# Block-sparse attention feeding a gated feed-forward layer: scores in array tiles of 64 rows from loaded queries, and another order inside a step

## The chip, the cores and the metric

The kernel runs on one core of one Trainium2 chip. The metric is device time in microseconds, from one launch of the whole program; lower is better. The kernel before was timed three times, with a median of 854.73 us (854.47 to 855.68). One further execution was recorded by the hardware profiler; all rows below are from that one.

## The reference

Attention over 4 batches, 8 heads, 768 positions and a head dimension of 64. Positions form 24 blocks of 32. A query block sees its own block and the two beside it, the first and the last block, and three sampled blocks; the first and the last query block see every key. What is not seen is masked before the softmax. The result goes through a feed-forward layer whose middle is `h * erf(softplus(h))`. All inputs are float32.

```python
scores = scale * np.matmul(q, k.transpose(0, 1, 3, 2))
mask = np.abs(blk_i - blk_j) <= 1
mask = mask | (blk_i == 0) | (blk_j == 0) | (blk_i == n_blocks - 1) | (blk_j == n_blocks - 1)
for qb in range(n_blocks):
    for kb in sampled_blocks[qb]:
        mask[qb * 32:(qb + 1) * 32, kb * 32:(kb + 1) * 32] = True
attn = softmax(np.where(mask, scores, -1e9))
x = (attn @ v), heads side by side            # 3072 tokens x 512
h = x @ w_in                                  # 512 -> 2048
sp = np.maximum(h, 0.0) + np.log1p(np.exp(-np.abs(h)))
out = (h * erf(sp)) @ w_out                   # 2048 -> 512
```

## The kernel before

**Units of attention.** The work on scores is cut into 16 units for each batch. Ten are of kind `m`: four query blocks (`t` from 0 to 4) for four heads (`quad` 0 or 1, two head pairs `r` each). Two are of kind `e`: the two query blocks before the last, again for four heads. Four are of kind `f`: the last and the first query block for one pair of heads (`pr`), against all 768 keys. The order in a batch is ten `m`, then f0, e0, f1, f2, e1, f3.

**Queries.** `load_q` brings the queries of four blocks into a tile `qt` of 128 rows: 64 rows of one head of a pair above 64 rows of the other. `order_q` copies them into `qm`, which was set to zero once: for each pair of heads and each block it holds 128 rows by 64 columns, one head's queries in the upper rows of 32 columns, the other's in the lower rows of the other 32, and zeros elsewhere. So one product over all 128 rows gives the scores of both heads.

**Scores.** In `scores`, an `m` unit makes 24 products: two head pairs, three groups of key columns (96 around the block, 96 gathered by GpSimd into `kg`, 64 of the first and last block), four blocks. Each writes 64 rows of the PSUM tile `s` (two banks, one buffer): blocks alternate between the upper and the lower 64. They are in float32, and the trace holds two weight loads and two matmuls for each product. An `e` unit makes 12 such products in one bank, an `f` unit two products of 512 and 256 columns with all 128 columns of the array.

**After the scores.** `soft_max` takes the row maxima on VectorE (`mx`, `nb`). `soft_exp` makes the exponentials on ScalarE (`pf`) and their float16 upper part, `soft_low` the lower part on VectorE (`p`). `soft_turn` has SyncE's queue turn them through DMA into `pT`. Two units later `values` multiplies them with the gathered values `vb` into `po` (one buffer): 96 products for an `m` place, 192 for the place of `f` and `e`, in four array tiles of 128 rows by 32 columns. `norm` divides on VectorE (`rinv`, `xf`). At each second place `turn` splits the result in two halves (ScalarE, then VectorE) and turns it by DMA into `xT` for the feed-forward layer.

**The feed-forward layer.** 96 groups: 12 chunks of 256 tokens by 8 groups of 256 columns. `ff_first` makes 24 matmuls of 256 columns into `h` (three buffers), `ff_logs` five passes on ScalarE, `ff_power` one on VectorE, `ff_exp` one on ScalarE, `ff_gate` three on VectorE (in the next step), `ff_second` twelve matmuls of 512 columns into `o` (two steps later).

**Order.** Every instruction stays in program order on its engine. A prologue works on the first four units while the weights are decoded. Then 98 steps follow. A table (`until`) says in which steps a unit is begun: in each of the first sixteen, after that in five or six of each eight. A step of before issues: products `h` and their passes; `values` of the unit two back; `gathers` (GpSimd copies of keys, SyncE loads of values, with block numbers that the engine reads first); `scores` and `used_keys`; `ff_gate`; `norm`; early work on the weights; `ff_second`; `soft_max`; `next_queries` (`order_q`, `load_q`); `ff_power`; `soft_exp`; `ff_exp`; stores; `turn`; `soft_low`; `soft_turn`. SyncE's queue is also in program order: within a step the loads of values, then that of queries, then the turns.

## Time and profile before

| What | Value |
|---|---|
| median of three runs | 854.73 us |
| the profiled execution's own time | 856.55 us |
| its span, from the first to the last instruction | 854.8 us |
| TensorE matmul busy | 712.1 us, 83% of the span, 11100 matmuls |
| TensorE weight loads busy | 505.2 us, 11100 loads |
| ScalarE busy | 601.0 us, 70% |
| VectorE busy | 553.7 us, 65% |
| GpSimd busy | 136.0 us, 16% |
| mean granted TensorE clock | 0.94 of full speed |

1.75 us of the execution's time lie outside its span. Busy matmul time counts the stretch from a matmul's start to a modelled end; matmuls overlap, so the time that a block takes is read from the start of one block to the start of the next. [...]

### The profile page before, as it was taken

The page shows a single profiled execution, that of the slowest core. Times are in us where ns is not written, and L with a number is a line of the kernel's source. Part 1 is how long each engine was busy: PE and PEld are TensorE (multiplying, and loading weights), DVE is VectorE, ACT ScalarE, POOL GpSimd, SP SyncE. Part 2 cuts the span into 40 slices and gives each one's busy share as a digit, 9 for nine tenths or more (in the row PEclk, how much of TensorE's full clock was granted, in tenths as well). Part 3 has the DMA queues.
Part 4 walks back from the last instruction along what each step waited for, and adds up shares of the span by engine and source line. Part 5 has one row for each costly group of instructions (what it writes and reads, how often), then busy time and mean ns, then how long its engine had stood idle before and what let it go on. Part 6 is the DMA issues. An engine that isn't in the chain of part 4 may idle for free.

```text
span 854.8 us, 26699 instructions
## 1 busy us (share of the span) xinstructions
PE 712.1 (83%) x11100; PEld 505.2 (59%) x11100; DVE 553.7 (65%) x974; ACT 601.0 (70%) x999; POOL 136.0 (16%) x350
## 2 busy tenths in 40 slices
PE   1224655877997999899999989899999899999997
PEld 1214543544675766666776666566767676666663
DVE  3947587677856466775657766766667667655453
ACT  4635556778877576796778777867777677776774
POOL 6514020111321123200113231000111100000000
PEclk9556776999999899999999999999999999999999
DMA  8986733666689988662589697831576867211000
GB/s 325 388 252 187 227 88 86 163 169 174 165 174 206 219 197 209 177 162 45 132 164 208 177 211 170 206 97 44 132 160 151 190 129 186 65 31 39 1 26 26
DMA packets 199930, 131.61 MB, mean 154 GB/s; under 512 B 144000, under 2 KB 167168, under 8 KB 199808
## 3 DMA queue, kind: packets, MB, share of 16 engines
q1 hardware_dynamic: 195520, 114.95, 55.1%
q0 software_dynamic: 4288, 14.95, 5.0%
q8 instruction: 87, 1.43, 0.7%
q14 instruction: 35, 0.29, 0.1%
HBM read 83.88 MB, written 12.95 MB: 113 GB/s over the span
## 4 chain that ended last, share of the span: by engine, by line
PE 43%; DVE 17%; ACT 13%; DMA 11%; issue 10%; SPq 2%; POOL 2%; POOLq 0%; ACTq 0%
PE h L52 17%; PE o L52 16%; PE po L52 4%; PE s_m L52 4%; ACT x L52 3%; ACT pf_m L52 3%; DMA vtab<-vn 3%; DVE mx_m L52 3%; DVE g L52 3%; DVE q L52 3%; DMA vb<-vtab 2%; ACT q L52 2%; SPq L52 2%; DVE p_m L52 2%; ACT p_m L52 2%
## 5 line engine op out<-in xcount | busy, mean ns | idle before, releaser
L52 PE MATMUL o<-wo,g 128*128 128x512 f16 x1152 | 271.0, 384 | 16.2 <-DVE wo L52 8.5
L52 PE MATMUL h<-xT,wi 128*128 128x256 f16 x2304 | 273.8, 276 | 12.4 <-DVE wi L52 8.3
L52 PEld LDWEIGHTS <-wi 128*128 128x128 f16 x2304 | 227.9, 99 | 62.6 <-DVE wi L52 9.2
L52 PEld LDWEIGHTS <-g 128*128 128x128 f16 x1152 | 110.2, 99 | 142.5 <-issue 24.6
L52 ACT ACTIVATE x<-x 128x512 f32<-128x512 f32 x288 | 181.5, 630 | 9.1
L52 POOL COPY kg<-kx 128x128 f32 x264 | 97.6, 422 | 281.7 <-PE s_m L52 176.6
L52 ACT ACTIVATE pf_m<-s_m,nb_m 128x256 f32<-128x256 f32 x160 | 62.8, 475 | 73.0 <-DVE nb_m L52 72.6
L52 DVE SCALAR_TENSOR_TENSOR q<-x,q 128x512 f32<-128x512 f32 x96 | 66.7, 694 | 61.4 <-ACT x L52 60.4
L52 ACT ACTIVATE x<-h,isg 128x512 f32<-128x512 f32 x96 | 65.3, 680 | 37.2 <-PE h L52 36.7
L52 PE MATMUL s_m<-kx,qm 128*64 128x64 f32 (+1 forms) x1280 | 74.9, 247 | 9.9 <-ACT pf_m L52 7.5
L52 ACT ACTIVATE q<-q 128x512 f32<-128x512 f32 x96 | 59.5, 619 | 29.8 <-DVE q L52 29.8
L52 DVE SCALAR_TENSOR_TENSOR q<-q,h 128x512 f32<-128x512 f32 x96 | 65.5, 682 | 22.6 <-ACT q L52 21.9
L52 DVE TENSOR_TENSOR p_m<-pf_m,p_m 128x1024 f16<-128x1024 f32 x40 | 49.3, 1233 | 38.0 <-ACT p_m L52 38.0
L52 PE MATMUL po<-vb,pT_m 128*32 128x65 f16 (+1 forms) x3840 | 43.9, 202 | 35.9 <-DMA vb<-vtab 24.2
L52 DVE SCALAR_TENSOR_TENSOR g<-q,g 128x512 f16<-128x512 f32 x96 | 66.5, 693 | 3.3
L52 PEld LDWEIGHTS s_m<-kx,qm 128*64 128x64 f32 x1280 | 59.6, 145 | 13.3 <-ACT pf_m L52 8.1
L52 PEld LDWEIGHTS <-pT_m 128*32 128x32 f16 x3840 | 38.0, 98 | 46.0 <-issue 19.0
L52 ACT ACTIVATE q<-x 128x512 f32<-128x512 f32 x96 | 60.5, 630 | 3.0
L52 DVE TENSOR_REDUCE mx_m<-s_m 128x4 f32<-128x1024 f32 x40 | 48.7, 1218 | 16.0 <-PE s_m L52 16.0
L52 PE MATMUL s_m<-kg,qm 128*64 128x96 f32 x640 | 47.7, 258 | 6.0 <-POOL kg L52 4.7
L52 DVE TENSOR_TENSOR x<-xf,x 128x512 f16<-128x512 f32 x24 | 17.1, 714 | 47.3 <-ACT x L52 47.3
L52 DVE TENSOR_SCALAR g<-q 128x512 f16<-128x512 f32 x96 | 41.4, 431 | 3.3
(111 smaller groups left out, 631.3 us busy)
## 6 DMA issues: line engine op xcount, KB each, us to landing
vb<-vtab SPq DMA_DIRECT2D x280, 65.0 KB, 2.9
vb<-vtab SPq DMA_DIRECT2D x32, 390.0 KB, 4.0
vraw<-in_v_dram SPq DMA_DIRECT2D x10, 768.0 KB, 5.2
wo<-in_w_out_dram POOLq DMA_DIRECT2D x14, 512.0 KB, 5.9
vtab<-vn SPq DMA_DIRECT2D x16, 390.0 KB, 5.6
vb<-vtab SPq DMA_DIRECT2D x12, 520.0 KB, 4.7
qt<-in_qT_dram SPq DMA_DIRECT2D x20, 256.0 KB, 3.7
out_dram<-wo SPq DMA_DIRECT2D x20, 256.0 KB, 3.9
```

Source lines behind the costliest of these rows:

```text
L52: done = call(*args, **kwargs)
```

## The change

Queries are no longer copied: `qm` with its zeros and `order_q` are gone, and `qt` has two buffers. `scores` takes each head of a pair by itself: 64 rows of `qt` (upper or lower) against 64 rows of keys, 32 queries wide (64 in an `f` unit). An `m` unit then makes 48 products in eight array tiles of 64 rows by 32 columns: the column place follows the block, the row half follows the head, and each half writes its own bank of `s`. An `e` unit makes 24 products, each pair of head and block with its own 32 rows of one bank; an `f` unit makes four, with a head's 64 rows each, both in the same banks. `values` reads its columns where the new layout puts them. `load_q` is called right after `scores`, in other units than before.

A step is also ordered otherwise. On TensorE: `h`, scores, `o`, values (before: `h`, values, scores, `o`). On VectorE: `ff_gate`, maxima, power, `soft_low`, `norm`, the split of `turn` (before: `ff_gate`, `norm`, maxima, `order_q`, power, the split of `turn`, `soft_low`). On SyncE's queue: the load of queries, the loads of values (which now follow later products), then the turns.

```diff
     qts = {}
-    qm = cp.tile([P, HP, 4, 2, BLOCK], F32, tag="qm", name="qm")
-    pool.memset(qm, 0.0)
 
     def load_q(b, t):
-        place, tag, bufs = (mo, "g", FF_LAG + 1) if b == 0 and t in (1, 2) else (ld, "qt", 1)
-        qt = place.tile([P, HP, P], F32, tag=tag, name=f"qt_{b}_{t}", bufs=bufs)
+        qt = ld.tile([P, HP, P], F32, tag="qt", name=f"qt_{b}_{t}", bufs=2)
...
-    def order_q(b, t):
-        qt = qts.pop((b, t)).rearrange("p r (j c) -> p r j c", c=BLOCK)
-        copy = act.copy if b == 0 and t in (1, 2) else dve.tensor_copy
-        for a in range(2):
-            copy(qm[a * D : (a + 1) * D, :, :, a, :], qt[a * D : (a + 1) * D])
...
-            s4 = s.rearrange("p (h r w) -> p h r w", h=2, r=2)
+            qt = qts[b, t]
+            s4 = s.rearrange("p (a r w) -> p a r w", a=2, r=2)
             for r in range(2):
                 pr = 2 * quad + r
                 for part in range(3):
                     for j in range(4):
-                        o = slice((j % 2) * 64, (j % 2) * 64 + 64)
-                        q_ = qm[:, pr, j].rearrange("p a c -> p (a c)")
-                        c, e, keys = key_columns(b, 1 + 4 * t + j, slice(0, P), pr)[part]
-                        pe.matmul(s4[o, j // 2, r, c:e], q_, keys, start=True, stop=True)
+                        o = slice(j * BLOCK, (j + 1) * BLOCK)
+                        for a in range(2):
+                            rows = slice(a * D, (a + 1) * D)
+                            c, e, keys = key_columns(b, 1 + 4 * t + j, rows, pr)[part]
+                            pe.matmul(s4[o, a, r, c:e], qt[rows, pr, o], keys, start=True, stop=True)
...
                     for j in range(2):
-                        o = slice(j * 64, j * 64 + 64)
-                        q_ = qm[:, 2 * quad + r, j].rearrange("p a c -> p (a c)")
-                        c, e, keys = key_columns(b, NB - 3 + j, slice(0, P), 2 * quad + r)[part]
-                        pe.matmul(s3[o, r, c:e], q_, keys, start=True, stop=True)
+                        for a in range(2):
+                            rows, o = slice(a * D, (a + 1) * D), j * 64 + a * BLOCK
+                            c, e, keys = key_columns(b, NB - 3 + j, rows, pr)[part]
+                            q_ = qt[rows, pr, j * BLOCK : (j + 1) * BLOCK]
+                            pe.matmul(s3[o : o + BLOCK, r, c:e], q_, keys, start=True, stop=True)
...
-            q_ = qm[:, pr, 2:].rearrange("p n a c -> p (n a c)")
             for c, e in ((0, 512), (512, S)):
-                keys = kxs[b][:, c // BLOCK : e // BLOCK, pr, :]
-                pe.matmul(s[:, c:e], q_, keys, start=True, stop=True)
+                for a in range(2):
+                    rows = slice(a * D, (a + 1) * D)
+                    keys = kxs[b][rows, c // BLOCK : e // BLOCK, pr, :]
+                    pe.matmul(s[a * 64 : a * 64 + 64, c:e], qts[b, MT][rows, pr, 64:], keys, start=True, stop=True)
...
     def next_queries(m):
 
         b, n = divmod(m, per)
-        if n < 10 and n % 2 == 1:
-            order_q(b, n // 2 + 1)
-            if n < 9:
-                load_q(b, n // 2 + 2)
-        if n == per - 1 and b + 1 < B:
-            order_q(b + 1, 0)
-            load_q(b + 1, 1)
+        if n in (1, 3, 5, 7):
+            load_q(b, n // 2 + 2)
+        elif n in (9, 15) and b + 1 < B:
+            load_q(b + 1, n // 15)
...
             ff_first(*group)
             ff_logs(*group)
+        if unit:
+            scores(unit)
+            used_keys(unit)
+            next_queries(begun - 1)
+        if last:
+            ff_gate(*last)
+        if m < len(EARLY):
+            work(EARLY[m])
+        if m >= FF_LAG:
+            for u in range(CT):
+                ff_second(*groups[m - FF_LAG], u)
         if place:
             values_of(place)
         if steps:
             gathers(begun)
         if unit:
-            scores(unit)
-            used_keys(unit)
-        if last:
-            ff_gate(*last)
-        if place:
-            norm(*place)
-        if m < len(EARLY):
-            work(EARLY[m])
-        if m >= FF_LAG:
-            for u in range(CT):
-                ff_second(*groups[m - FF_LAG], u)
-        if unit:
             soft_max(unit)
-            next_queries(begun - 1)
...
+        if unit:
+            soft_low(unit)
         if place:
+            norm(*place)
             turn(*place)
         if unit:
-            soft_low(unit)
             soft_turn(unit)
```

## Rows read from the trace of the kernel before

**Rows 1.** The page's second part: the span in 40 equal slices, busy share of TensorE and its granted clock, in tenths.

```profile
PE   1224655877997999899999989899999899999997
...
PEclk9556776999999899999999999999999999999999
```

**Rows 2.** Busy time of each engine in stretches of the span: stretch, length, then for TensorE, its weight loads, VectorE, ScalarE and GpSimd busy us (instructions), granted clock, DMA share, GB/s.

```profile
96.00:236.00 140.00, 101.81 (x1551) 69.59 (x1551) 100.64 (x163) 99.51 (x161) 21.42 (x58) 0.87 0.56 149
236.00:310.00 74.00, 63.66 (x1272) 47.92 (x1270) 44.95 (x85) 50.10 (x89) 15.72 (x43) 0.95 0.86 193
310.00:484.00 174.00, 165.49 (x2605) 117.64 (x2604) 115.34 (x215) 132.31 (x226) 28.47 (x72) 1.00 0.69 164
785.00:855.00 70.00, 63.66 (x424) 41.03 (x421) 31.80 (x54) 43.83 (x69) 0.00 (x0) 1.00 0.07 20
```

**Rows 3.** The chain of waits that ended last, in order of time, one full step: start us, us, what. The length is that from one block to the next.

```profile
640.67 2.62 PE h L52 x24
643.29 0.89 PE po L52 x94
644.18 1.98 PE s_m L52 x48
646.16 2.69 PE o L52 x12
648.86 2.62 PE h L52 x24
```

**Rows 4.** TensorE in order of time around one `m` block of scores: start us, us to the end of the last, operation, out and in, shape of the array tile and of the output, count.

```profile
409.01 0.55 PE L52 MATMUL s_m<-kx,qm 128*64 128x96 f32 x8
409.39 0.50 PE L52 MATMUL s_m<-kg,qm 128*64 128x96 f32 x8
409.72 0.73 PE L52 MATMUL s_m<-kx,qm 128*64 128x64 f32 x16
410.28 0.50 PE L52 MATMUL s_m<-kg,qm 128*64 128x96 f32 x8
410.94 0.39 PE L52 MATMUL o<-wo,g 128*128 128x512 f16 x1
```

**Rows 5.** The same view in the products with values of an `f` and `e` place, where the program issues f, e, e, f six times, then f, f twelve times, and then the next head again f, e, e, f.

```profile
421.64 0.48 PE L52 MATMUL po<-vb,pT_f 128*32 128x65 f16 x20
421.94 0.20 PE L52 MATMUL po<-vb,pT_e 128*32 128x65 f16 x1
```

**Rows 6.** The same view around an `f` block of scores, and the busy time of the scores of each kind between 236 and 785 us (columns as in rows 2, without GpSimd; first `m`, then `f`, then `e`).

```profile
374.26 1.46 PE L52 MATMUL s_f<-kx,qm 128*128 128x512 f32 x4
375.55 2.75 PE L52 MATMUL o<-wo,g 128*128 128x512 f16 x12
...
236.00:785.00 549.00, 65.86 (x1440) 59.49 (x1440) 36.57 (x30) 47.08 (x120) 0.99 0.65 150
...
236.00:785.00 549.00, 17.77 (x48) 8.17 (x48) 11.41 (x12) 10.66 (x12) 0.99 0.65 150
...
236.00:785.00 549.00, 7.82 (x144) 6.75 (x144) 4.12 (x6) 5.04 (x12) 0.99 0.65 150
```

**Rows 7.** ScalarE in order of time in one step whose block `h` ends at 651.4 us: start us, us, operation, count, and in brackets the idle time before it and what ended that.

```profile
651.51 0.69 ACT L52 ACTIVATE x<-h,isg 128x512 f32<-128x512 f32 x1 [0.61 <-PE h L52]
655.87 1.57 ACT L52 ACTIVATE pf_m<-s_m,nb_m 128x256 f32<-128x256 f32 x4 [1.01 <-DVE nb_m L52]
657.47 1.06 ACT L52 ACTIVATE p_m<-pf_m 128x1024 f16<-128x1024 f32 x1
658.43 0.61 ACT L52 ACTIVATE q<-q 128x512 f32<-128x512 f32 x1
```

**Rows 8.** Groups of instructions: operation, out and in, shapes, count, then busy us and mean ns of one, then idle us before it and what ended most of that.

```profile
L52 DVE TENSOR_TENSOR p_m<-pf_m,p_m 128x1024 f16<-128x1024 f32 x40 | 49.3, 1233 | 38.0 <-ACT p_m L52 38.0
L52 DVE TENSOR_TENSOR xf<-po,rinv 128x256 f32<-128x256 f32 x48 | 20.4, 424 | 1.7
L52 DVE RECIPROCAL rinv<-rinv 128x4 f32<-128x4 f32 x48 | 8.6, 178 | 1.7
L52 DVE TENSOR_SCALAR rinv<-po 128x4 f32<-128x4 f32 x48 | 7.5, 157 | 28.5 <-PE po L52 28.5
L52 DVE COPY qm<-qt 64x512 f32<-64x512 f32 x44 | 19.9, 451 | 0.7 <-DMA qt<-in_qT_dram 0.4
L52 ACT ACTIVATE x<-xf 128x512 f16<-128x512 f32 x24 | 14.8, 615 | 2.2 <-DVE xf L52 2.2
```

**Rows 9.** Who waited for whom: waits in all (the first line, over the span), then TensorE's own between 310 and 705 us. Columns: us in total, times, longest us.

```profile
ACT pf_m L52 <- DVE nb_m L52: 72.6, 35, 9.0
...
PE po L52 <- DMA pT_m<-p_m: 7.2, 4, 2.8
PE s_f L52 <- ACT pf_m L52: 2.2, 2, 2.0
```

**Rows 10.** SyncE's queue in order of time: start us, us, operation, count (the time between two lines goes to register reads and waits).

```profile
660.41 8.37 SPq L52 DMA_DIRECT2D vb<-vtab  x15
668.88 0.40 SPq L52 DMA_DIRECT2D qt<-in_qT_dram  x1
669.37 1.25 SPq L52 DMA_TRANSPOSE xT<-x  x1
670.74 2.92 SPq L52 DMA_TRANSPOSE pT_m<-p_m  x1
```

More of the change, by code (lines that the diff above doesn't have):

```diff
@@ L563, in scores @@
             (quad,) = n
+            qt = qts[b, MT]
             s3 = s.rearrange("p (r w) -> p r w", r=HP)
             for r in range(2):
+                pr = 2 * quad + r
                 for part in range(3):
                     for j in range(2):
-                        o = slice(j * 64, j * 64 + 64)
-                        q_ = qm[:, 2 * quad + r, j].rearrange("p a c -> p (a c)")
-                        c, e, keys = key_columns(b, NB - 3 + j, slice(0, P), 2 * quad + r)[part]
-                        pe.matmul(s3[o, r, c:e], q_, keys, start=True, stop=True)
+                        for a in range(2):
[3 more added lines that the diff above has]
+                            pe.matmul(s3[o : o + BLOCK, r, c:e], q_, keys, start=True, stop=True)
             softs[unit] = (s[:, :512], 2, 256)
@@ L596, in values @@
                         if t < MT:
-                            pT = pts["m", b, t, quad][:, ((j // 2) * 2 + r) * 4 + x * 2 + half]
-                            col = (j % 2) * 64 + a * 32
+                            pT = pts["m", b, t, quad][:, (a * 2 + r) * 4 + x * 2 + half]
+                            col = j * BLOCK
                             vg = vb[:, slot_of[b, 1 + 4 * t + j]]
@@ L609, in values @@
                         for j in (0, 3):
-                            pT, col = pts["f", b, pr][:, x * KT + k], (0 if j else 64) + a * 32
+                            pT, col = pts["f", b, pr][:, x * KT + k], a * 64 + (32 if j == 0 else 0)
                             w = slice(c, c + D + 1) if ln == 0 else slice(c + D + 2, c + VW)
@@ L795, in behind @@
             c = b + 1
-            if n == 10:
-                load_q(c, 0)
             k = n if b else 2 * (n - 10) if n > 9 else -1
@@ L859, in sparse_attention_moe @@
     load_q(0, 1)
-    load_q(0, 2)
     for n in range(3):
@@ L869, in sparse_attention_moe @@
     place_v(0, 1, 1)
-    order_q(0, 0)
     have_k.add(0)
@@ L896, in sparse_attention_moe @@
     used_keys(units[1])
+    next_queries(1)
     gathers(0)
@@ L901, in sparse_attention_moe @@
     soft_exp(units[1])
-    order_q(0, 1)
     work("Qi1 Di2 Qi2 Di3 Qi3")
@@ L919, in sparse_attention_moe @@
     used_keys(units[3])
+    next_queries(3)
     gathers(0)
@@ L927, in sparse_attention_moe @@
     soft_exp(units[3])
-    order_q(0, 2)
     work("Qo0 Do1 Bi Hi0 Qo1")
@@ L941, in sparse_attention_moe @@
     gathers(0)
-    load_q(0, 3)
     begun = FIRST
```

## The prediction

> **What bounds the kernel now.** I read the 40 slices first: from the eleventh on TensorE is at 9 tenths almost everywhere, at full clock; before that it is not, and the clock is half or a little over [rows 1]. The table by stretches says the same in numbers: from 310 to 484 us TensorE is busy 165.5 of 174 us at clock 1.00, ScalarE 132.3, VectorE 115.3; from 96 to 236 us TensorE has 101.8 of 140, ScalarE 99.5, VectorE 100.6, and none is full [rows 2]. After 785 us only `h` and `o` are left. Busy matmul time overlaps itself, so I then took the chain of waits: a step with an `m` unit is `h` 2.62, values 0.89, scores 1.94 to 1.98, `o` 2.69, one behind the other with no wait, 8.2 us in all [rows 3]. So from 236 to 785 us a microsecond less in a block of TensorE is a microsecond less of time, as long as the other engines follow. That stretch holds 30 `m` blocks (1440 matmuls by 48), 12 `f` blocks (48 by 4) and 6 `e` blocks (144 by 24) [rows 6]. The ten earlier `m` units stand where TensorE waits for others.
>
> **The `m` block.** It runs from 409.01 to 410.94, 1.93 us. Eight matmuls of 96 columns take 0.33 us (409.39 to 409.72); eight of 64 and eight of 96 take 0.56, so eight of 64 take 0.23 [rows 4]. Over six times eight that gives 4 x 0.33 + 2 x 0.23 = 1.78, and 0.15 remain for the start and the way to `o`. Two run at a time: the array tile has 64 columns. In the new block there are 96 matmuls of the same lengths, 32 columns wide on 64 rows, on eight places. If all eight places work together, the stream is 96 / 8 = 12 slots instead of 48 / 2 = 24, so 0.89 us. The two matmuls of one product follow each other on the same place, so the first slot is only half used: one slot more, 0.08. With the 0.15 that is 1.12 us, and 0.81 less a block; 30 x 0.81 = **24.3 us less**.
>
> Whether the engine keeps eight places busy depends on whether it passes over a matmul whose place is taken. It does: after the first head's run of f, f, products of e start at 421.94 when 20 f have started in that run, while the program has 24 f before them (and two more f that frame e) [rows 5]. So it looks some matmuls ahead. Four places at once are shown by the values (96 products in 0.89 us [rows 3]), in float16 and over all rows. Row halves are not shown anywhere: every matmul of this trace uses 128 rows. The bounds are therefore 0.89 of stream (eight at a time) and 3.56 (two at a time, as the scores run now: 48 slots); between them lies 1.78 (four at a time, as the values run). I take eight, because the values already show one stream for each column place and the halves read other rows and, in `m`, write another bank.
> [...]
>
> **The `f` and `e` blocks.** An `f` block takes 1.29 us (374.26 to 375.55) [rows 6]. Its four products take two column places, each on its own row half: half as many at a time as products doubled, so the same stream. An `e` block has twice the products on four places instead of two: the same.
>
> **Changes of the array's tile.** The last eight matmuls of 64 columns begin at 410.61 (0.33 after 410.28) and end their 0.23 at 410.84, `o` begins at 410.94: 0.10 for one change [rows 4]. Before, a step with values and an `m` block has three changes; now scores and values are apart and it has four. That is 0.10 in the 27 `m` steps that have values (nine a batch, three batches) and in 6 `e` steps. An `f` block had none of its own (374.26 follows `h` directly) and now has two: 12 x 0.20. Together 2.7 + 0.6 + 2.4 = **5.7 us more**.
>
> **The copies.** 44 copies of 0.451 us on VectorE, 19.9 us, and four on ScalarE are gone [rows 8]. VectorE is not the bound after 236 us; its other work covers them. Before that it alternates with ScalarE. There I take 2 us less, with bounds of none and 10 (the ten units' copies and the shorter blocks in full). The load of queries now waits for the scores alone, not for the copy; behind it on SyncE's queue are the loads of values and the turns, and the scores end early in the step, so nothing waits longer.
>
> **The new order on ScalarE and VectorE.** Before, ScalarE has ended its five passes over `h` 1.01 us before 655.87 and waits for `nb` [rows 7]; over the span that wait is 72.6 us [rows 9]. Now the scores end 0.1 + 1.1 us after `h`, not 2.9, and `norm` no longer stands before the maxima: `nb` is there before the passes end, and this wait goes. What is late next is `turn`: its ScalarE copy (0.615) needs `norm`, which now stands behind `soft_low` on VectorE. From the end of `p` that is 1.23 + 0.16 + 0.18 + 0.42 = 2.0 us [rows 8]; only `ff_exp` (0.61) lies beside it [rows 7]. ScalarE, with the next group's passes queued behind the copy, waits 1.4 us at every second place, 18 times from 236 us on: 25 us if nothing hides it. What hides it: the 1.0 us that is saved at each of the two units, and the steps without a unit, where TensorE needs 2.6 + 2.6 us and ScalarE some 4 (its passes from 651.51 to 654.86 and 0.61 for `ff_exp` [rows 7]). I take **3 us more**; bounds 0 and 25.
>
> **The values and SyncE's queue.** Values come 1.1 + 2.6 us later after `h`. That covers waits of values for turned scores (7.2 us between 310 and 705 us [rows 9]). Against it, the loads of values follow the values: 15 issues took 8.4 us in a row, and behind them stand the turns of `x` and `p` (1.25 and 2.92) [rows 10]. They move back by the same 3.7 us, while two shorter steps bring the need 1.4 us nearer. I take **3 us less**, bounds 7 less and 6 more.
>
> **Sum.** Against the profiled execution's own 856.55 us (span 854.8 and 1.75 around it): -24.3 + 5.7 - 2 + 3 - 3 = -20.6, so 836. That execution is 1.8 us above the median of the runs, 854.73; the forecast in its terms is **834 us**, 2.4% faster.
>
> **Rivals.**
> *Row halves take turns* (slower): a matmul on one row half doesn't start while the other half of its column place streams. Then four run at a time, the `m` stream is again 1.78, the 24.3 fall away and the 5.7 stay: 858. It decides from the first `m` block; for it: no row shows halves together; against it: their rows, weights and, in `m`, banks are apart. It is also the case in which the change doesn't do what it says.
> *Two at a time* (slower): float32 streams, which read twice the bytes of the values' float16, stay at two, as in rows 4. The `m` stream is 3.56, 1.78 more in 30 blocks, 0.89 more in 6 `e` blocks, some 5 us in the earlier units: 858 + 53 + 5 + 5 = 921. Against it: nothing shows that two is more than the number of places that a 64-column tile leaves.
> *The wait at `turn` shows by half*: 12.5 in place of 3, so 844. For it: where three units follow each other no step without a unit helps; ScalarE is busy 132 of 174 us [rows 2], and steps get shorter.
> *One bank for both halves*: in `e` and `f` blocks both halves write one bank, which no row of before has with other rows of the array. If they take turns there, `f` grows by 1.29 (12 times) and `e` by 0.89 (6 times): 15.5 + 5.3 more, 855. [...]
>
> **Chances.** Forecast 0.58 (own range 820 to 846, from the bounds of the three smaller terms), wait at `turn` 0.15, row halves in turns 0.11, one bank 0.09, two at a time 0.07. The range 817 to 858 holds the first, third and fourth rivals' times and leaves out two at a time, half of what lies about 858, and the tails of the forecast. 0.2%, 1.7 us, is about what a measurement can tell from no change. Faster: nearly all of the first two and less than half of one bank, 0.77; same 0.06; slower 0.17.
>
> **What would show it.** In the changed kernel's trace, the `m` block on TensorE lasts about 1.1 us with eight matmuls of 96 columns starting within some 80 ns; `f` stays at 1.3 plus two changes; the wait of `pf_m` for `nb` nearly vanishes; ScalarE's copy of `turn` waits about 1.4 us for `xf`; the step with values and an `m` unit goes from 8.2 to 7.5 us. An `m` block of 1.9 us or more makes the forecast wrong, and so do short blocks with new idle time of TensorE in front of them.

## The result and the profile after

The changed kernel takes 863.66 us (median of four runs, 862.21 to 866.10) against 854.99 for the kernel before on the same chip: ratio 1.0088, 95% interval 1.0060 to 1.0115. It is slower by 0.9%, where 2.4% faster was forecast; the time lies above the upper end of the range, 858. The profiled execution took 866.1 us. Its page, with the lines that answer to [rows 1] and the table before:

```profile
span 864.4 us, 31004 instructions
...
PE 702.4 (81%) x13276; PEld 467.3 (54%) x13276; DVE 538.6 (62%) x930; ACT 598.9 (69%) x995; POOL 129.6 (15%) x349
...
PE   1315645768988788999998987899999999999997
...
PEclk9997756899999998999999999999999999999999
...
q8 instruction: 104, 1.70, 0.8%
q14 instruction: 34, 0.28, 0.1%
```

TensorE has 2176 matmuls more and is busy 10 us less, in a span that is 10 us longer: the slices between the eleventh and the twenty-fifth hold more eights and sevens than before. The last two lines are queues that bring instructions (packets, MB); they matter further down.

TensorE in order of time around an `f` and an `m` block of scores (columns as in [rows 4, 6]):

```profile
411.46 1.51 PE L52 MATMUL s_f<-kx,qt 64*64 64x512 f32 x8
412.90 2.77 PE L52 MATMUL o<-wo,g 128*128 128x512 f16 x12
415.50 2.78 PE L52 MATMUL h<-xT,wi 128*128 128x256 f16 x24
418.21 0.40 PE L52 MATMUL s_m<-kx,qt 64*32 64x96 f32 x16
418.40 0.37 PE L52 MATMUL s_m<-kg,qt 64*32 64x96 f32 x16
418.57 0.58 PE L52 MATMUL s_m<-kx,qt 64*32 64x64 f32 x28
...
419.46 2.77 PE L52 MATMUL o<-wo,g 128*128 128x512 f16 x12
```

Sixteen matmuls of 96 columns start within 0.19 us, so all eight places work at once. The `m` block takes 1.25 us to the start of `o`, where [rows 4] had 1.93, and the `f` block 1.44, where [rows 6] had 1.29. The tiles do what they were forecast to do, if not quite as much: 1.12 us was forecast for the `m` block.

The loss is in TensorE's waits and in what comes with them. Its own waits between 236 and 790 us:

```profile
PE o L52 <- DVE g L52: 11.1, 7, 2.4
PE po L52 <- issue: 8.3, 6, 2.8
PE po L52 <- DMA pT_m<-p_m: 7.2, 5, 2.1
PE s_m L52 <- ACT pf_m L52: 3.4, 3, 2.0
PE po L52 <- DMA vb<-vtab: 3.0, 5, 1.1
```

Before, the same list has no wait of `o` for `g` at all, and its line of `po` for issue is

```profile
PE po L52 <- issue: 1.9, 2, 1.1
```

And ScalarE's waits over the span (columns as in [rows 9]):

```profile
ACT x L52 <- PE h L52: 52.9, 49, 5.4
ACT x L52 <- DVE xf L52: 34.3, 23, 3.5
ACT pf_m L52 <- DVE nb_m L52: 28.4, 21, 5.4
```

The wait for `nb_m` has gone from 72.6 us [rows 9] to 28.4 (after 236 us from 49.5 to 4.8), and ScalarE's copy of `turn` now waits for `xf` 23 times, 1.5 us each (after 236 us 18 times, 25.9 us); it waited 2.2 us in all before [rows 8]. Both were forecast.

To keep a saving in blocks apart from waits, I counted each trace in the same way. From the first `h` of the steps on, every block of TensorE counts with its undisturbed length from one block's start to the next (`h` 2.62, `o` 2.59, values 0.89 and 2.27, scores `m` 1.94 or 1.24, `f` 1.29 or 1.44, `e` 1.04 or 1.02). What is left is called waiting here. It is split into stalls for instructions (explained with e1), the rest in the first sixteen steps, and the rest after them. Some 6 us of each span lie behind the last block. All in us, with a few records missing from each trace:

```
kernel     first h   blocks   stalls   waits, steps 1-16   waits later   sum
before      96.2     649.2      9.3          54.4             39.2       848
after       95.3     626.2     14.4          63.5             58.7       858
e1          96.1     626.2     62.2          54.8             34.1       873
e2          96.9     649.2     13.2          59.7             50.4       869
e3          95.5     626.2     12.7          58.4             64.0       857
e4          94.7     626.2     64.3          59.6             46.1       891
e13         96.0     625.0     19.0          53.6             46.5       840
e16         99.2     647.2     10.1          49.9             44.6       851
```

From before to after the blocks fall by 23.0 us. Stalls take back 5.1, waits in the first sixteen steps 9.1, later waits 19.5: together 33.7, so the kernel loses 10. (In e13 and e16 one block of scores stands ahead of the first `h`.)

Not all that is called waiting is idle time. From the first `h` to the last block TensorE's granted clock reads 0.5, the lower of the two values that it takes in these traces (1.0 and 0.5), for 45 us before and for 78 us after. An `h` at 96.2 us of before, over which it reads 0.54 in the mean, takes 4.85 us to the next block in place of 2.62. Weighed with TensorE's busy time in these stretches, that makes its blocks some 16 us longer before and some 29 after (an estimate from the two traces). Each of the seven falls after 236 us in the changed kernel's trace comes in or just behind a wait of TensorE (2.0 to 2.8 us). The stretch from 96 to 236 us, with a clock of 0.87 in [rows 2], now reads

```profile
96.00:236.00 140.00, 98.66 (x1876) 61.83 (x1875) 95.42 (x151) 96.91 (x156) 19.16 (x49) 0.81 0.57 146
```

Changes of the array's tile count as waits too. An `h` lasts 2.71 us to the next block where scores of the new tiles or values follow it and 2.62 where `o` does, an `o` 2.69 ahead of values and 2.59 ahead of `h` (medians of the traces). The change adds some 6 us of these. So of the 28.6 us by which the waits grow, some 13 are the lower clock, some 6 changes of the tile, and some 10 idle time.

### The profile page after: what moved, and what is told of

It reads as the page before. It is cut to its first block, busy times and chain, and to the rows that moved or that the text cites. A ratio compares the mean times of both kernels' runs of the same rounds, so it can differ in the third digit from the quotient of the medians.

```text
span 864.4 us, 31004 instructions
## 1 busy us (share of the span) xinstructions
PE 702.4 (81%) x13276; PEld 467.3 (54%) x13276; DVE 538.6 (62%) x930; ACT 598.9 (69%) x995; POOL 129.6 (15%) x349
## 5 line engine op out<-in xcount | busy, mean ns | idle before, releaser
L52 PE MATMUL o<-wo,g 128*128 128x512 f16 x1152 | 281.9, 395 | 32.3 <-ACT wo L52 12.4
L52 PE MATMUL h<-xT,wi 128*128 128x256 f16 x2304 | 277.3, 278 | 12.7 <-DVE wi L52 8.8
L52 PEld LDWEIGHTS <-wi 128*128 128x128 f16 x2304 | 225.6, 100 | 56.5 <-DVE wi L52 9.8
L52 POOL COPY kg<-kx 128x128 f32 x264 | 92.2, 398 | 408.4 <-PE s_m L52 311.6
L52 ACT ACTIVATE pf_m<-s_m,nb_m 128x256 f32<-128x256 f32 x160 | 62.5, 473 | 29.2 <-DVE nb_m L52 28.4
L52 PE MATMUL s_m<-kx,qt 64*32 64x96 f32 (+1 forms) x2560 | 57.3, 252 | 13.5 <-ACT pf_m L52 12.4
L52 PEld LDWEIGHTS s_m<-kx,qt 64*32 64x32 f32 x2560 | 43.3, 110 | 22.8 <-ACT pf_m L52 14.5
L52 ACT ACTIVATE p_m<-pf_m 128x1024 f16<-128x1024 f32 x40 | 42.3, 1057 | 1.5 <-ACT pf_m L52 0.2
L52 PE MATMUL s_m<-kg,qt 64*32 64x96 f32 x1280 | 37.9, 258 | 6.2 <-POOL kg L52 3.6
```

The costliest lines, as they stand in the source:

```text
L52: done = call(*args, **kwargs)
```

## The experiments

In all of them the new tiles go with the loaded queries, the old ones with `qm` and its copies. Each kernel was timed against the kernel before on the same chip; ratios are to that. The diffs are against the changed kernel unless another is named. Lists of waits have the columns of [rows 9].

### e1 to e4: the change taken apart

e1 has the tiles alone, in the step order of before:

```diff
+        if place:
+            values_of(place)
+        if steps:
+            gathers(begun)
         if unit:
             scores(unit)
...
-        if place:
-            values_of(place)
-        if steps:
-            gathers(begun)
...
-        if unit:
-            soft_low(unit)
         if place:
-            norm(*place)
             turn(*place)
         if unit:
+            soft_low(unit)
             soft_turn(unit)
```

(`norm` goes behind `ff_gate` again.)

> The new score tiles and loaded queries alone, in the step order of before (products h, values, gathers, scores, then gates, norm, maxima; turn ahead of soft_low). Theory A (norm and turn behind soft_low on VectorE cost what the tiles gain): 836 us, since of the forecast's sum the terms of the m block, the tile changes and the copies stay (-24.3 + 5.7 - 2, against 855). Theory B (the place of the scores and of o on TensorE costs it, because o comes sooner after h than its gate is ready): also 836. Theory C (ScalarE and VectorE bound the step whatever TensorE does, so the shorter block turns into waits in any order): 853, between 850 and 857. In all three the m block to the next block is 1.2 us.

Measured: 886.18 us, ratio 1.0321 (1.0285 to 1.0356). All three theories are wrong: the tiles alone make the kernel slower by far more than the whole change does. TensorE's waits between 236 and 790 us, and then one unit in order of time:

```profile
PE s_m L52 <- issue: 44.2, 23, 2.9
PE po L52 <- DMA pT_m<-p_m: 5.0, 5, 2.2
```

```profile
336.47 1.05 PE L52 MATMUL po<-vb,pT_m 128*32 128x65 f16 x96
337.45 0.40 PE L52 MATMUL s_m<-kx,qt 64*32 64x96 f32 x16
...
337.90 0.48 PE L52 MATMUL s_m<-kx,qt 64*32 64x64 f32 x21
341.22 0.28 PE L52 MATMUL s_m<-kx,qt 64*32 64x96 f32 x4 [2.85 <-issue]
...
341.85 4.45 PE L52 MATMUL o<-wo,g 128*128 128x512 f16 x12
```

In the middle of a block of scores TensorE stands for some 3 us, and waits for no other engine. "Issue" means that nothing the profile shows holds it back. What holds it back is its supply of instructions. The page of the changed kernel above gives the sizes (e1 has the same matmuls and as many packets): the queue for instructions brought 104 packets with 1.70 MB, so 16 KB each, and a second such queue 0.28 MB; together 1.98 MB for 31004 instructions is 64 bytes an instruction, so a packet holds 256. 104 times 256 is 26624, and TensorE has 26552 matmuls and weight loads; before, 87 times 256 is 22272 for 22200. So this queue feeds TensorE. Its line in the page of before:

```profile
q8 instruction: 87, 1.43, 0.7%
```

I counted TensorE's instructions in order of their start: of 34 gaps of over 0.6 us inside a block after 230 us, 27 end at a count that leaves 193 when divided by 256. A piece of instructions ends there. Six such pieces in a row, around the stall shown:

```
count at the   piece took   stall behind   packet starts after    TensorE goes on after
piece's end        us          it, us       the piece begins       the packet has landed
  9153            2.86          2.01             2.44                     1.32
  9409           13.86          0.02             3.98                     8.94
  9665            1.48          3.09             1.71                     1.59
  9921           12.95          0.00             3.04                     9.03
 10177            1.33          1.23             0.24                     1.33
 10433            6.34          0.00             1.44                     3.93
```

The packet for the next piece starts while the present one is worked through, lands about 1 us later (in the changed kernel a packet takes 1.03 us, the median of 104), and TensorE goes on 1.2 to 1.6 us after that. A piece that lasts 6 us hides this, one that lasts 1.4 does not. Over the whole trace after 230 us: 26 pieces took up to 2 us, and 25 of them were followed by a stall of over 0.3 us, 52 us in all; of the 52 that took over 3.2 us none was. Behind the stall shown, `o` takes 4.29 us to the next block in place of 2.59: from 341.2 to 345.5 us the granted clock is 0.61 in the mean. The new `m` block has 96 matmuls and 96 loads, the values as many; in the order of before they stand side by side, 384 instructions in 2.1 us, so a piece can run out within them. With the old tiles it was 288 in 2.8 us.
Nor is a longer piece always safe. In the changed kernel six of the 76 pieces of over 3.2 us were followed by stalls of 0.5 to 1.7 us, and in e13 seven of 3.8 to 3.9 us by stalls of 0.3 to 3.9; there the packet started 1.4 to 5.3 us after the piece began. What sets its start was not found.

e2 is the other half: the new order with the scores of before.

```diff
-            qt = qts[b, t]
-            s4 = s.rearrange("p (a r w) -> p a r w", a=2, r=2)
+            s4 = s.rearrange("p (h r w) -> p h r w", h=2, r=2)
...
         if unit:
             soft_max(unit)
+            next_queries(begun - 1)
```

> The other half alone: the new step order with the scores of before (qm, diagonal, copies of queries behind the maxima). Theories A and B: the order by itself costs what the tiles would have given, about 15 to 20 us, so 870 (862 to 880). Theory C: the order is about neutral by itself, 852 to 858.

Measured: 873.84 us, ratio 1.0170 (1.0140 to 1.0200), as A and B expected: the order by itself costs 15 us. In the table that is 11 us of later waits, 5 in the first steps and 4 of stalls; by the same estimate some 12 us of these waits are the lower clock and 4 changes of the tile (one trace of each kernel). Among TensorE's waits the first line is again the gates:

```profile
PE o L52 <- DVE g L52: 12.9, 8, 2.4
```

e3 puts `norm` and `turn` ahead of `soft_low` in the changed kernel:

```diff
-        if unit:
-            soft_low(unit)
         if place:
             norm(*place)
             turn(*place)
         if unit:
+            soft_low(unit)
             soft_turn(unit)
```

> The changed kernel with norm and turn put before soft_low on VectorE and ScalarE; the order on TensorE and on SyncE's queue stays the new one, except that the turn of x is ahead of nothing new. Theory A: ScalarE's copy no longer waits 1.5 us for xf, 34 us of that wait go, and the time is 840 (835 to 846). Theory B: 860 (856 to 864), the wait of o for the gate stays at 11 us or more between 236 and 790 us. Theory C: 855 to 863, with the wait moved to soft_turn.

Measured: 863.88 us, ratio 1.0053 (1.0027 to 1.0079). Against 1.0088 that is some 3 us better, and the two intervals overlap. The wait that the forecast named is thus there, but in this order of TensorE it isn't what costs most of the time; theory A falls. `o` still waits 14.1 us for gates.

e4 leaves `norm` and `turn` behind `soft_low` and puts the products with values back ahead of the scores:

```diff
+        if place:
+            values_of(place)
+        if steps:
+            gathers(begun)
         if unit:
             scores(unit)
...
-        if place:
-            values_of(place)
-        if steps:
-            gathers(begun)
```

> The changed kernel with values and gathers put back ahead of the scores (TensorE and SyncE's queue as before the change), norm and turn left behind soft_low on VectorE. Theory A: 858 (854 to 864), ScalarE's copy still waits 1.5 us for xf some 20 times. Theory B: 842 (836 to 848), the wait of o for the gate falls from 11 us to under 3 between 236 and 790 us. Theory C: 853 to 858.

Measured: 901.16 us, ratio 1.0522 (1.0477 to 1.0568). No theory had that: the stalls are back (64 us in the table), and on top of e1 the late `norm` and `turn` cost 15 us; the next products with values, among others, wait until `norm` has read `po`:

```profile
PE s_m L52 <- issue: 47.6, 23, 2.9
PE po L52 <- DVE xf L52: 6.4, 5, 2.0
```

So the two halves of the change belong together in a way that the forecast missed. The order puts `o`, 24 instructions in 2.6 us, between the two dense blocks, and keeps away most of the stalls that the tiles would bring (64.3 us in e4, 14.4 in the changed kernel); and it costs waits of its own (11 us of later waits in e2).

### e7, e10, e11: the stalls taken away otherwise

These leave out two of the three terms of the products with values, in e1 (e7), in the changed kernel (e10) and in the kernel before (e11):

```diff
-            for x, ln in ((0, 0), (0, 1), (1, 0)):
+            for x, ln in ((0, 0),):
```

> The kernel e1 with two of the three terms of the products with values left out (the lower parts of p and of v do not enter: 32 products instead of 96 in an m place, 64 instead of 192 in the other), so that values and scores together are 256 of TensorE's instructions and no longer 384. Theory F (TensorE gets its instructions in pieces of 256, and a piece gone through in under 2 us is followed by a stall, since the next one has not come yet): the stalls inside the blocks of scores, 44.2 us in e1, fall to under 8, and with 25 us of products gone (0.5 in 30 places, 1.4 in 7) the time is 820 (813 to 832). Rival K (tiles of 64 rows are slow behind products with values, whatever their number): the stalls stay, 861 (855 to 867).

> The changed kernel with the same two terms of the products with values left out as in e7 (the lower parts of p and of v do not enter). Theory F: it had few stalls to lose, so it gains at most the 25 us of products and loses some to ScalarE: 842 (836 to 852), and so it is slower than e7, while with all terms it is 22 us faster than e1. Rival K: 839, and faster than e7.

> The kernel before with the same two terms of the products with values left out as in e7 and e10 (the lower parts of p and of v do not enter): the base for e7, which is this kernel with the new tiles and in which nearly no stall of instructions is left. Theory B (TensorE bounds the step in the old order too, so without the stalls the tiles give what the sum of TensorE's blocks says): 25 us of products and most of its 8 us of stalls go, then e7 lies 15 to 20 us below this one, which is at 848 to 852. Theory L (behind TensorE the chain from scores over softmax and turn by DMA to the products with values two units later is nearly as long, so that what TensorE saves there turns into waits): this one is at 830 to 836, within 5 us of e7.

Measured: e7 831.80 us, ratio 0.9679 (0.9630 to 0.9729); e10 834.45, 0.9695 (0.9657 to 0.9734); e11 830.12, 0.9660 (0.9626 to 0.9695). By the ratios e1 loses 55 us by the cut, of which the products are 25; the changed kernel loses 34, the kernel before 29. The tiles are the same as in e1, and the scores' wait for issue has gone from 44.2 us to 0.8, with 1.0 us of stalls by the count. This bears out theory F, at the upper edge of its range: the number of instructions makes the stalls, not the tiles of 64 rows (K had 861). e10 came out below F's range (836 to 852), and that e7 lies below e10 can't be told from no difference. e11 is where theory L had it; B had 848 to 852.

e11 shows the second thing: with no stalls in either, the new tiles (e7) bring nothing over the old ones. TensorE's waits between 236 and 790 us in e7:

```profile
PE po L52 <- DMA pT_m<-p_m: 13.9, 5, 4.0
PE po L52 <- DMA vb<-vtab: 5.7, 5, 4.3
PE s_m L52 <- POOL kg L52: 4.7, 8, 1.3
PE s_f L52 <- ACT pf_m L52: 4.2, 2, 2.5
...
PE s_m L52 <- issue: 0.8, 1, 0.8
```

In e11 the first of these is

```profile
PE po L52 <- DMA pT_m<-p_m: 6.4, 3, 2.6
```

and the next three are 3.9, 5.4 and 2.5. The blocks are 23 us shorter (618.6 in e11, 595.7 in e7) and the later waits 18 us longer (44.6 and 62.8; the lower clock has only some 1 us of that, by the estimate above): turned scores, gathered values and the one buffer of `s`, all of which come two units or one unit behind TensorE, are late instead. This fits theory L as to the place, not yet as to its cause.

### e6, e18, e8, e12: single cures of the order

e6 gives the gates one step more: `FF_LAG = 3` in place of 2 in the changed kernel.

> The changed kernel with the second product three steps behind the first, not two (a fourth buffer for the gates, one step more at the end); nothing else. Theory G (in the new order o follows h by 1.2 us instead of 2.8, so VectorE's gate of the step before is late): the 11.1 us in which o waits for g between 236 and 790 us fall to under 1, and the time is 850 (845 to 856). Rival H (ScalarE and VectorE cannot keep up anyway, the wait moves to the scores or to h): 860 to 865.

Measured: 875.20 us, ratio 1.0156 (1.0108 to 1.0203). The wait of `o` for `g` is gone, as G said, but the time got worse, by more than H had. Scores wait for the exponentials instead, and by the count of the table the stalls are 7 us and the waits in the first sixteen steps 4 us longer than in the changed kernel:

```profile
PE po L52 <- issue: 11.3, 12, 2.8
PE s_f L52 <- ACT pf_m L52: 11.0, 2, 5.6
```

e18 computes the gate in its own step:

```diff
-        if last:
-            ff_gate(*last)
...
         if unit:
             soft_low(unit)
+        if group:
+            ff_gate(*group)
         if place:
             norm(*place)
```

> The changed kernel with VectorE's gate of a group in the group's own step, between soft_low and norm, and no longer at the start of the next. Theory V (in the changed kernel VectorE's gate stands behind norm, which waits for products with values, and behind the split of turn, which waits for ScalarE's copy; this queueing costs, not the work): the wait of o for g (11.1 us between 236 and 790 us) and the wait of h or scores behind it go, 852 (846 to 858). Rival W (norm and turn come later by the gate's 1.9 us and the turned rows or the scores take over the wait): 862 to 870.

Measured: 883.40 us, ratio 1.0287 (1.0243 to 1.0331), worse than even W. `o` waits 4.3 us for `g`, and the scores 26 us for exponentials:

```profile
PE s_m L52 <- ACT pf_m L52: 15.1, 5, 4.8
PE s_f L52 <- ACT pf_m L52: 11.3, 2, 6.2
```

e8 is e1 with values and gathers ahead of `h`:

```diff
+        if place:
+            values_of(place)
+        if steps:
+            gathers(begun)
         if group:
             ff_first(*group)
             ff_logs(*group)
```

> The kernel e1 with the products with values and the gathers put at the start of the step, ahead of h; ScalarE and VectorE keep the order of before (norm behind the gate, turn ahead of soft_low). On TensorE values and scores are now kept apart by h and by o, as in the changed kernel. Theory F: the wait of the scores for issue falls from 44.2 us to under 5; o is as near to h as in the changed kernel and waits for gates 8 to 14 us; 858 (852 to 866). Rival K2 (the old order of norm and turn does not go with the new tiles): 875 to 886.

Measured: 877.34 us, ratio 1.0201 (1.0161 to 1.0241). The scores' wait for issue falls to 5.7 us, near the 5 that F had. But the values now come before their turned scores are there, and the gates, which F had late by 8 to 14 us, are not late at all. The time is the one of K2; its reason was not tried by itself:

```profile
PE po L52 <- DMA pT_m<-p_m: 22.0, 8, 4.5
PE po L52 <- issue: 8.8, 7, 2.2
```

e12 is a third order: scores, `h`, values, `o` on TensorE, with the exponentials of the scores ahead of the passes over `h`:

```diff
+        if unit:
+            scores(unit)
+            used_keys(unit)
+            next_queries(begun - 1)
         if group:
             ff_first(*group)
-            ff_logs(*group)
...
+        if unit:
+            soft_exp(unit)
+        if place:
+            norm(*place)
+        if group:
+            ff_logs(*group)
```

> The changed kernel in a third order: scores at the start of the step, then h, values, o, so that the two dense blocks are kept apart by h and by o; ScalarE makes the exponentials of the scores before the five passes over h; VectorE: maxima, gates, norm, soft_low, the split of turn, power. Theory F alone (pieces of instructions and TensorE's blocks decide): under 8 us of stalls inside scores, and 840 (834 to 848). Theory L: the stalls are as few, but the gates and the exponentials come later on a ScalarE that has no time to spare, and the time is 855 to 870.

Measured: 868.73 us, ratio 1.0110 (1.0072 to 1.0148). It has few stalls (11.9 us by the count) and gates nearly in time (3.8 us), but `o` waits 16.5 us until VectorE has copied the finished results out of it, and ScalarE waits 66.9 us for VectorE's power. The time is within the range of theory L.

Four cures, and in each a wait goes and another comes. None of the waits that were taken away one at a time is the cause by itself.

### e14, e15: is ScalarE short of time?

Both leave out the second Ln of `ff_logs` (the middle of the feed-forward layer is then another function), in the changed kernel and in the one before:

```diff
-        act.activation(x, x, AF.Ln, bias=1.0, scale=C4)
```

> The changed kernel with one of ScalarE's five passes over h left out (the second Ln; so the middle of the feed-forward layer is another function): 96 passes of 0.63 us, 60 us of ScalarE. Theory L (ScalarE's and VectorE's chain takes what TensorE saves): the saving comes through, 838 (828 to 846), below e15. Rival T (TensorE's blocks and its stalls for instructions alone make the time): 860 (856 to 864), above e15.

> The kernel before with the same pass of ScalarE left out (the second Ln). Theory L: it gains too, but less, since TensorE's blocks are longer here: 846 (840 to 852). Rival T: 852 (848 to 856).

Measured: e14 860.86 us, ratio 1.0034 (1.0006 to 1.0062); e15 850.58, 0.9936 (0.9908 to 0.9965). ScalarE loses 60 us of work and each kernel some 5 by the ratios: what T expected, within 2 us, and e14 stays above e15. So it is not ScalarE's load that takes the saving, and that part of theory L falls.

### e13 and e16: an order in which the engines block each other less

e13 is e12 with three moves, each against a wait seen in e12:

```diff
+        if last:
+            ff_exp(*last)
         if group:
             ff_first(*group)
...
             for u in range(CT):
                 ff_second(*groups[m - FF_LAG], u)
+            for u in range(CT):
+                ff_store(*groups[m - FF_LAG], u)
         if unit:
             soft_low(unit)
-        if place:
-            turn(*place)
         if group:
             ff_power(*group)
-            ff_exp(*group)
+        if place:
+            turn(*place)
```

> The kernel e12 with three moves against its waits: the last pass over h (ff_exp) goes to the start of the next step on ScalarE, so that ScalarE no longer waits for VectorE's power (66.9 us in e12); the stores of results stand ahead of soft_low, so that o no longer waits for them (16.5 us in e12); power stands ahead of the split of turn. Theory L (what counts beside TensorE is when ScalarE and VectorE come round in a step; an order with slack for the gates and without ScalarE's waits lets TensorE's saving through): 845 (836 to 853), faster than both kernels. Rival: the exponentials of the scores and the turns wait for a slot on the DMA queues or the values (po for vb and pT grow from 8 us to over 20), 858 to 868.

Measured: 848.29 us, ratio 0.9912 (0.9881 to 0.9944): faster than both kernels. No work was added or left out, only the order differs from the changed kernel's. Its page and TensorE's waits between 236 and 790 us:

```profile
span 846.3 us, 30992 instructions
...
PE 698.0 (82%) x13276; PEld 467.7 (55%) x13276; DVE 535.2 (63%) x930; ACT 600.3 (71%) x995; POOL 133.0 (16%) x349
```

```profile
PE po L52 <- issue: 13.3, 8, 3.7
PE po L52 <- DMA pT_m<-p_m: 10.8, 5, 4.3
PE po L52 <- DMA vb<-vtab: 4.8, 5, 2.6
PE s_m L52 <- ACT pf_m L52: 3.5, 3, 1.6
```

Gates are down to 1.0 us; what is left is led by stalls for instructions inside the values.

e16 has e13's order with the old scores, in the manner of e2.

> The order of e13 with the scores, the diagonal and the copies of queries of before (tile of 64 columns over 128 rows). Theory S (the tiles' saving on TensorE is real and comes through where the order neither puts both dense blocks together nor blocks an engine): 20 us slower than e13, about 866 (860 to 874). Theory Q (e13 gains by its order alone; the tiles bring nothing in any order): within 5 us of e13, 844 to 853.

Measured: 855.54 us, ratio 0.9958 (0.9929 to 0.9988). It lies between the theories: the third order alone brings about 3 us, and the tiles in it another 4 by the ratios or 7 by the medians. The intervals of e13 and e16 overlap, so the tiles' part is only just told from nothing, and it is far from the 20 us of theory S. By the table the blocks are 22 us shorter in e13 than in e16, stalls take back 9 of that and waits 6.

## Why the prediction failed

**The premise.** The sum rests on "a microsecond less in a block of TensorE is a microsecond less of time, as long as the other engines follow". They did not follow. In each order that was run with both kinds of tiles the new ones shorten the blocks by 22 to 23 us, and the time goes down by 7 us in the new order (e2 and the changed kernel, by the ratios), by 4 in the third (e16 and e13), not at all in the old one without stalls (e11 and e7), and up by 27 in the old one with them (e1). The prediction's own sign against itself, short blocks with new idle time of TensorE in front of them, is what the trace shows.

**The `m` block, 24.3 us less.** Right in kind. The block went from 1.94 to 1.24 us (median of 30, start to next start), not 1.12, so 21 us less. All eight places work together.

**Changes of the tile, 5.7 more.** About right: some 6 us from 236 us on. The `f` block has 1.44 us where it had 1.29, the `e` block 1.02 where it had 1.04; the rest is in `h` ahead of scores and in `o` ahead of values, which the table counts as waits. Blocks as a whole fell by 23 us over all units (ten of the 36 `m` blocks stand in the first sixteen steps).
The `f` and `e` blocks write one bank from both row halves, on other partitions, and their streams are not longer: with its changes of the tile `f` takes 1.44 us and `e` 1.02, where the rival "one bank" had 2.58 and 1.93. It was wrong.

**The copies, 2 less.** Not borne out in the stretch it was meant for: waits in the first sixteen steps grew by 9.1 us, in e2, which keeps the copies, by 5.3, and in e1, which has none and the old order, by 0.4; most of the 9.1 is the lower clock (some 7 us by the estimate above). What the copies cost by themselves was not run.

**The new order on ScalarE and VectorE, 3 more (bounds 0 and 25).** This is the step that failed. The event was foreseen to the tenth: ScalarE's copy waits 1.5 us for `xf`, where 1.4 was worked out, and after 236 us it does so 18 times for 25.9 us, the forecast's count and its whole 25 us. What was wrong is the argument that steps without a unit and the 1.0 us saved at each unit would hide it, and that this wait was the one that matters. The order alone costs 15 us (e2), and the wait for `xf` only some 3 of what the changed kernel loses (e3). Nor does the "own range 820 to 846" come out of the bounds that it names: with 0, 25 and 6 us at the upper end the sum reaches 867, above what was measured. One step, ScalarE and then VectorE in order of time:

```profile
644.69 0.61 ACT L52 ACTIVATE q<-q 128x512 f32<-128x512 f32 x1
646.82 0.63 ACT L52 ACTIVATE x<-xf 128x512 f16<-128x512 f32 x1 [1.52 <-DVE xf L52]
647.35 0.67 ACT L52 ACTIVATE x<-h,isg 128x512 f32<-128x512 f32 x1
```

```profile
644.82 1.23 DVE L52 TENSOR_TENSOR p_m<-pf_m,p_m 128x1024 f16<-128x1024 f32 x1 [1.68 <-ACT p_m L52]
645.96 0.15 DVE L52 TENSOR_SCALAR rinv<-po 128x4 f32<-128x4 f32 x1
...
647.48 0.69 DVE L52 TENSOR_TENSOR x<-xf,x 128x512 f16<-128x512 f32 x1 [0.70 <-ACT x L52]
648.09 0.68 DVE L52 SCALAR_TENSOR_TENSOR q<-q,h 128x512 f32<-128x512 f32 x1
```

VectorE stands 1.68 us for ScalarE's upper half, ScalarE 1.52 for VectorE's `xf`, VectorE 0.70 for ScalarE's copy, and only then, at 648.09, comes the gate whose input ScalarE had ready at 645.3. The forecast followed one engine to the wait and stopped there; each engine's wait stood in the other's queue. That this ring of waits makes up the 15 us is argued from such steps, not shown: e3 takes `norm` and `turn` ahead in it and gains some 3 us, e18 takes the gate out of it and loses. And TensorE asks earlier: `o` follows `h` by 1.24 us and no longer by 2.83, so late gates show, 11.1 us. That they are a sign and not the cause fits e6, where they are in time and the kernel is slower, but e6 has more stalls too.

**Values and SyncE's queue, 3 less.** About right as far as it went: values wait 7.2 us for turned scores where it was 8.1, and 3.0 for gathered values where it was 6.0. Not foreseen: they wait 8.3 us for issue, where it was 1.9.

**What no step had: the clock.** The forecast counted on the full clock from 236 us on. After the change it reads 0.5 for 24 us behind that point, where it was 10 us before; with the first steps the lower level costs some 13 us more than before, by the estimate above.

**What no step had: instructions.** The forecast counted 96 matmuls in place of 48 by their stream alone. Their number alone would have cost 53 us of stalls in the old order (62.2 against 9.3), more than the tiles save. The new order, which the forecast took for a small cost and nothing else, is what avoids most of that.

**The rivals.** "Row halves take turns", "two at a time" and "one bank" are refuted by the blocks (`m` 1.24 us, where the first two have 1.78 and 3.56 for its stream alone; `f` 1.44 and `e` 1.02). "The wait at `turn` shows by half" named a wait that came in full on ScalarE, but by e3 it is worth some 3 us and not 12.5; the rest of the loss is not its own. None named the true combination.

**What stays open.** Why e7 gains nothing over e11 is known by place (turned scores, gathered values, the buffer of `s`) and not to a single cause; ScalarE's load is ruled out as one. Which of e13's three moves brings most of the 17 us (by the ratios) from e12 to e13 was not tried one by one. What makes a packet of instructions start late, and how much of the lower clock would go with the waits, is open too.

## What to carry to other kernels

When a change doubles the number of short matmuls, count TensorE's instructions as well as their stream: look in the trace for gaps inside a block that wait for issue, and keep two dense blocks apart by one of few, long matmuls (here 62.2 us of stalls in e1, 14.4 with `o` between them). A saving on one engine is worth what the next deadlines leave of it (here 22 to 23 us less in the blocks were worth 7 us, 4, nothing, and once cost 27): after a block is shortened, the engines that serve it must deliver earlier, so follow each queue in program order through both engines until nothing waits, not just to the first wait. Read the granted clock beside the waits: here the lower level made up some 13 of the 28.6 us by which they grew. And try the order again with the new lengths; here that turned 0.9% slower into 0.9% faster with the same instructions.

## What the hardware showed that was not expected

TensorE takes in its instructions in pieces of 256 (104 packets of 16 KB for 26552 matmuls and weight loads, the changed kernel), and a piece worked through in up to 2 us was followed by a stall in 25 of 26 cases, up to 3.15 us, mostly 1.2 to 3 (e1); longer pieces, too, were followed by stalls where the packet started late, 1.4 to 5.3 us after the piece began (six of 76 in the changed kernel, stalls of 0.5 to 1.7 us; seven of 3.8 to 3.9 us in e13, stalls of 0.3 to 3.9). The same instructions stalled for 64.3 us or 14.4, with nothing moved but the products with values and their gathers (e4 and the changed kernel). Float32 matmuls on 64 rows by 32 columns ran on all eight places, 16 of 96 columns starting in 0.19 us, and where two row halves write other partitions of one bank their streams ran together (`e` 1.02 us against 1.04 before, `f` 1.44 against 1.29, a change of the tile included).
